# Attention with filler: the value products of two steps in one group, and the place of the maxima next to them

## The chip, the cores and the metric

The kernel runs on one core of a Trainium2 chip. The core has five engines with a queue each: TensorE (PE in the profile; its weight loads are shown as PEld), VectorE (DVE), ScalarE (ACT), GpSimd (POOL) and SyncE (SP, which here only issues DMAs). The metric is the device time of one execution in microseconds (us); less is better.

## The reference: what is computed

Four layers in turn on a sequence of 2048 rows of 448 numbers, each with a residual: attention, gated unit, attention, gated unit, with the same weights both times.

```python
x = x + A(layernorm(x)); x = x + B(layernorm(x)); x = x + A(layernorm(x)); x = x + B(layernorm(x))

def A(x):          # 16 query heads of 28, one key and value head for all
    q = (x @ wq) in 16 heads;  k = x @ wk;  v = x @ wv
    p = softmax(q k^T * 28 ** -0.5);  o = p v
    return o (heads side by side) @ wo
def B(x):          # F = 1792
    return (sigmoid(x @ w_gate) * (x @ w_up)) @ w_down
```

## The kernel before, in words

One attention and one gated unit make a *layer* of the kernel (`l` is 0 or 1). In a layer the queries are cut into 16 *units* of 128 rows (`u`), the keys into 16 blocks of 128 (`kt`). A **step** is one unit with one key block, so a layer has 256 steps, 16 to a unit. An order of letters, `ORDER` (line 901), says what a step issues, and in which order:

- `S`: `scores` (lines 506 to 514), four times a step, once for each group `g` of four heads. One matmul s of 96 rows into a bank of PSUM (L510), then ScalarE's exponential of it into an SBUF tile P of 128 x 512 in 32 bits (L513). Eight P tiles take turns.
- `P`: `pv` (lines 516 to 526): the products of the four P tiles of the *step before* with the values. Four matmuls stand side by side in four column strips of 32 (L521), all into one bank "pv" that sums over the 16 key blocks. Each of the four shows as two records in the profile, since the operands have 32 bits. After the last block of a unit ScalarE copies the bank out (L525).
- `M`: one step of `mx_gen` (lines 463 to 504), which works one unit ahead: four matmuls in four row strips of 32 (L480) and four reductions on VectorE (mp, L484), which give the maxima of the scores in advance. Once a unit, two small VectorE operations (L493, L494), a transpose on TensorE (mt, L499), a copy (L501) and a DMA on POOL's queue (L502) put the maxima into the query tile QS, from which the scores of the next unit are computed. It also issues the loads of QH and QS on SP.
- `X`: the side work of finished units (`tick`, stages f0 to ff of `Block.tile`, and db to df of `down`): the division by the sums with its DMAs, the product with wo (12 matmuls, L612), the layernorm, and in the first layer the keys and values of the next (kv). It also sets `rate`, the filler planned per step: what is left, over the steps until it must be done.
- `F`: `fill.slice(rate / number of F)`: filler from a generator, counted by a price per matmul (110 for the gated unit's gp and up, 190 for its down product dn, 216 for the query projection qp). The generator takes matmuls until the price is used up; side work (wo, kv) is charged to the same account, so after a wo some slices are empty. Each slice also issues deferred work (evictions on ScalarE and VectorE) that has become due.

The order of every engine's queue is the order of the program, so the letters set it. Between the layers, and after the last, a loop of filler slices with side work runs without scores. Scores, maxima, filler results and transposes share seven PSUM banks (tag "f", `fps`); a new tile takes the bank that was given back first. The eighth bank is pv's. A block of the gated unit is two units: it makes seven h tiles (`glu`, gp and up products, L345, tanh and products on ScalarE and VectorE), and then two down products read them. `HB` (ten) is the number of h tiles, and of the tiles with that tag that hold the first loads of x at the start (`load_x0`, line 794); `oT` (line 600) holds the divided output before wo, in two buffers.

Of the kernel before, what the change touches and what calls it, by code (L numbers as in the profile page):

```python
# [8 lines left out]
F32 = mybir.dt.float32  # L9
F16 = mybir.dt.float16  # L10
# [9 lines left out]
def interleaved_layers_kernel(ctx: ExitStack, tc: tile.TileContext, x, wq, wk, wv, wo, wg, wu, wd, out, layers=2):  # L20
# [7 lines left out]
    _, S, D = x.shape  # L28
    F = wg.shape[1]
    H, Dh = 16, 28  # L30
    NT, NB, G, KT, FC = S // 128, S // 512, H // 4, S // 128, F // 128
    U = NT
    TB, WB, HB = 2, 4, 10
    NBL = NT // TB
    EPS = 1e-5

# [5 lines left out]
    wk1 = ctx.enter_context(tc.tile_pool(name="wk1", bufs=2))  # L42
# [113 lines left out]
    def prep_q():  # L156
        parts = wk1.tile([128, 4], F32, name="parts", bufs=1)
        for c in range(4):
            junk = wk1.tile([128, D], F32, tag="P", name="junq", bufs=8)
            squares(parts[:, c:c + 1], rq[:, c], junk)  # L160
        nc.vector.tensor_reduce(mxa[:, 2:3], parts, axis=AX.X, op=OP.add)
        nc.vector.memset(WQ[:, :, :, :, Dh:32], 0.0)
        yield
        yield from scales(mxa[:, 2:3], 1, pwa[:, 2:3], swa[:, 2:3])
        for c in range(4):
            r = rq[:, c].rearrange("p (h d) -> p h d", d=Dh)
            split(WQ[:, 0, c, :, 0:Dh], WQ[:, 1, c, :, 0:Dh], r, swa[:, 2:3])
            yield
        nc.vector.tensor_scalar(esc, pwa[:, 2:3], pwa[:, 0:1], None, op0=OP.mult)
        nc.vector.tensor_scalar(esc, esc, Dh ** -0.5 * 2.0 ** -14, None, op0=OP.mult)  # L170
# [336 lines left out]
    def scores(l, u, kt, g, P):  # L507
        assert ("m", l, u) in stored, (l, u, kt)
        s = psf.tile([128, 512], F32, tag=BANKS["s"], name="s", bufs=NBK[BANKS["s"]])
        nc.tensor.matmul(s, KK[l][0:96, 0, kt * 128:(kt + 1) * 128], QS[l, u][:, g].rearrange("p h n -> p (h n)"),  # L510
                         start=True, stop=True)
        p = wk1.tile([128, 512], F32, tag="P", name="P", bufs=8)
        nc.scalar.activation(p, s, AF.Exp, scale=esc)  # L513
        P.append(p)

# [32 lines left out]
    class Block:  # L548
# [8 lines left out]
        def tile(self, u):  # L557

            l, b = self.l, self.b
            t = u % TB  # L560
            v = {}

            def f0():
                v["o"] = PVS.pop((l, u))
                nc.sync.dma_start(sums[u % 2], v["o"][28:128:32])
                v["xr"] = wk1.tile([128, D], F32, tag="xr", name="xr", bufs=4)
                nc.sync.dma_start(v["xr"], x[0, u * 128:(u + 1) * 128] if l == 0 else x2d[u])
                return
                yield

            def fx():
                v["rc"] = wk1.tile([128, 16], F32, name="rc")
                nc.sync.dma_start(v["rc"], sums[u % 2].rearrange("g (a b) -> (g a) b", b=16))
                return
                yield

            def fy():
                nc.vector.reciprocal(v["rc"], v["rc"])
                return
                yield  # L580

            def fz():
                nc.sync.dma_start(sums[u % 2].rearrange("g (a b) -> (g a) b", b=16), v["rc"])
                return
                yield

            def fw():
                lb = v["lb"] = wk1.tile([128, 512], F32, name="lb", bufs=1)
                for g in range(G):
                    nc.sync.dma_start(lb[32 * g:32 * g + 32], sums[u % 2][g:g + 1].to_broadcast([32, 512]))  # L590
                return
                yield

            def fa():
                nc.gpsimd.tensor_tensor(v["lb"], v["o"], v["lb"], op=OP.mult)  # L595
                return
                yield

            def fb():
                oT = v["oT"] = wk1.tile([128, 2, 512], F16, name="oT")  # L600
                nc.scalar.copy(oT[:, 0], v["lb"])
                defer(lambda: nc.vector.tensor_tensor(oT[:, 1], v["lb"], oT[:, 0], op=OP.subtract))  # L602
                return
                yield

            def fc():
                need(1)
                p = fps([128, D], F32, "wo")
                n = 0
                for h in range(4):  # L610
                    for a, c in ((0, 0), (0, 1), (1, 0)):
                        nc.tensor.matmul(p, v["oT"][:, a, h * 128:(h + 1) * 128], WO[:, c, h], start=n == 0, stop=n == 11)  # L612
                        n += 1
                        yield C448

                def f():
                    nc.vector.scalar_tensor_tensor(self.x1[:, t], p, osc, v["xr"], op0=OP.mult, op1=OP.add)
                    v["ls"] = ln_stats(self.x1[:, t])[0]
                defer(f)

            def fd():
                if t == TB - 1:
                    self.load_w(0)
                    self.load_w(1)
                v["hl"] = ln_split(self.x1[:, t], *v["ls"], eng=nc.gpsimd)
                return
                yield

            def fe():
                if t == 0:  # L630
                    self.XT2 = wk1.tile([128, 7, TB * 128], F16, name="XT2")
                t7_dma(v["hl"], self.XT2, t)
                return
                yield

            def ff():
                self.fed += 1
                if self.fed == TB:
                    fill.add(self.bulk(), BULK)
                    if b == NBL - 1 and not self.last:  # L640
                        fill.add(qgen(l + 1, 1), G * QCH)
                return
                yield
            return (1, f0), (1, fx), (1, fy), (1, fz), (1, fw), (1, fa), (1, fb), (2, fc), (2, fd), (3, fe), (2, ff)

        def load_w(self, f):
# [135 lines left out]
    fill = Filler()  # L782
# [115 lines left out]
        nmx += 1  # L898

    early[0] = False  # L900
    ORDER = "FSFSFSFSPXM"
    MORE = (5, 10)
    FIRST = KT * TB + 16
    KEEP = 28000
# [1 line left out]
    for l in range(layers):  # L906
        mx = mxs[l]
        final = l + 1 == layers
        if not final:
            layer_tiles(l + 1)  # L910
        if l:
            for b in range(2, NB):
                fill.add(qgen(l, b), G * QCH)
        fill.slice(QCH)
        flush(True)
        next(mx, None)
        while late:
            late.pop(0)[1]()
        fill.slice(QCH)
        prevP = None  # L920
        rate = 0.0
        for step in range(U * KT):
            u, kt = divmod(step, KT)
            P = []
            for o in ORDER:
                if o == "S":
                    scores(l, u, kt, len(P), P)
                elif o == "M":
                    for _ in range(1 + (u == 0 and kt in MORE)):
                        next(mx, None)  # L930
                elif o == "P":
                    if prevP is not None:
                        pv(*prevP)
                elif o == "X":
                    if u and kt == 1:
                        b = (u - 1) // TB
                        if (l, b) not in BLK:
                            BLK[l, b] = Block(l, b)
                        later(*BLK[l, b].tile(u - 1))
                    if l == 0:  # L940
                        paced(step)
                    tick()
                    fed = sum(BLK[l, b].fed == TB for b in range(NBL) if (l, b) in BLK)
                    if fed < NBL - 1:
                        rate = fill.left / max(FIRST + TB * KT * fed - step, 1)
                    else:
                        rate = max(fill.left - KEEP, 0) / (U * KT - step)
                else:
                    fill.slice(rate / ORDER.count("F"))
            prevP = (l, u, kt, P)  # L950
        pv(*prevP)
        flush(True)
        later(*BLK[l, NBL - 1].tile(U - 1))
        if not final:
            mxs[l + 1] = mx_gen(l + 1)
        n = done = 0
        while (side or pend or fill.gens) if final else (side or pend or done < 4 * NB):
            tick()
            for _ in range(4):
                fill.slice(VS / 4)  # L960
            n += 1
            if not final and done < 4 * NB and QDONE.get((l + 1, 0)) == G and mx_ready(l + 1, done):
                if n >= 5 or done >= 4 * (NB - 1):
                    next(mxs[l + 1])
                    done += 1
                    n = 0
# [21 lines left out]
```

## Time and profile before

| | before |
|---|---|
| median of 3 runs (lowest to highest) | 2358.69 us (2357.77 to 2359.82) |
| the profiled execution's own time | 2358.22 us |
| its span, first to last instruction | 2356.4 us |
| mean granted TensorE clock | 0.985 |
| filled steps, first layer | about 268 to 1144 us of the span |
| between the layers | about 1146 to 1275 us |
| filled steps, second layer | about 1425 to 2269 us |

Times in the profile count from the first instruction. A row of the timeline gives the start, the time from the first start to the last end, engine, line, operation, output and inputs, size and count; in brackets stands idle time before it and what ended it. A row of a window gives for each engine the busy time and, in brackets, the instructions, then the granted clock, the DMA engines' busy share and GB/s. Matmuls overlap in the array: one starts while the one before still drains, so the time that a matmul costs is read from start to start.

### The profile page before, as it was taken

What the parts mean: (1) busy time and instruction counts of PE and PEld (TensorE: products, weight loads), DVE (VectorE), ACT (ScalarE), POOL (GpSimd) and SP (SyncE); (2) the same over time, 40 slices, a digit from 0 to 9 for tenths busy, and PEclk for the clock granted to TensorE, in tenths of its full rate; (3) what the DMA queues carried; (4) which work ended last, traced back from release to release, by engine and by line L of the source; (5) the groups of instructions that cost most, each with busy time, mean ns of one, the idle gap of its engine ahead of it and who ended that gap; (6) DMA issues with size and microseconds to landing.
All of it is one profiled execution on the core that took longest, in us unless ns stands there. A gap on an engine that the chain in (4) does not pass through costs nothing.

```text
span 2356.4 us, 41206 instructions
## 1 busy us (share of the span) xinstructions
PE 2239.1 (95%) x15736; PEld 1003.2 (43%) x15736; DVE 1635.5 (69%) x2917; ACT 1559.2 (66%) x2598; POOL 336.8 (14%) x602
## 2 busy tenths in 40 slices
PE   5888899999999999999998989999999999999999
PEld 3322243444444444444572224444444444444456
DVE  6888787777777777773358877867676777777321
ACT  5588676776667677677413777767676776767751
POOL 5203763100110110001101011000000000000010
PEclk9799999999999999999998999999999999999999
DMA  3244652323313132333342112222231313223133
GB/s 114 65 126 124 201 190 81 90 73 98 96 58 109 58 93 70 94 92 78 96 139 53 27 49 92 87 78 83 62 103 58 98 55 101 76 82 94 57 111 119
DMA packets 208071, 213.88 MB, mean 91 GB/s; under 512 B 139952, under 2 KB 168304, under 8 KB 207872
## 3 DMA queue, kind: packets, MB, share of 16 engines
q1 hardware_dynamic: 202496, 196.36, 28.5%
q0 software_dynamic: 5376, 14.87, 1.8%
q8 instruction: 123, 2.02, 0.4%
q14 instruction: 76, 0.62, 0.1%
HBM read 175.37 MB, written 23.59 MB: 84 GB/s over the span
## 4 chain that ended last, share of the span: by engine, by line
PE 51%; DVE 5%; DMA 1%; ACT 1%; issue 0%; SPq 0%; POOL 0%; ACTq 0%; DVEq 0%; POOLq 0%
PE pv L521 12%; PE s L510 10%; PE dn L702 8%; PE gp L345 7%; PE up L345 7%; DVE mp L484 4%; PE mx L480 4%; PE wo L612 2%; PE qp L345 1%; ACT P L513 0%; DMA sums<-rc 0%; DMA KK<-ktl 0%; DMA rc<-sums 0%; DMA sums<-pvs 0%; DVE st L297 0%
## 5 line engine op out<-in xcount | busy, mean ns | idle before, releaser
L513 ACT ACTIVATE P<-s,esc 128x512 f32<-128x512 f32 x2048 | 1307.8, 690 | 509.2 <-PE s L510 492.1
L484 DVE TENSOR_REDUCE mp<-mx 128x1 f32<-128x512 f32 x2048 | 1267.2, 681 | 412.2 <-PE mx L480 408.1
L510 PE MATMUL s<-QS,KK 96*128 96x512 f16 x2048 | 761.1, 381 | 52.7 <-DVE mp L484 34.8
L345 PEld LDWEIGHTS <-wgu 128*128 128x128 f16 x4928 | 458.6, 98 | 241.3 <-issue 94.5
L521 PE MATMUL pv<-P,VV 128*32 128x512 f32 x4096 | 547.3, 607 | 0.0
L345 PE MATMUL up<-XT,wgu 128*128 128x256 f16 x2464 | 375.6, 272 | 0.8 <-DVE mp L484 0.8
L345 PE MATMUL gp<-XT,wgu 128*128 128x256 f16 x2464 | 375.2, 274 | 0.2
L702 PE MATMUL dn<-WD,h 128*128 128x448 f16 x1344 | 321.7, 352 | 0.0
L510 PEld LDWEIGHTS <-KK 96*128 96x128 f16 x2048 | 194.5, 97 | 172.1 <-issue 93.0
L480 PE MATMUL mx<-KK,QH 32*128 32x512 f16 x2048 | 223.2, 392 | 20.7 <-ACT QH L402 4.8
L480 PEld LDWEIGHTS <-QH 32*128 32x128 f16 x2048 | 53.5, 91 | 396.5 <-issue 378.1
L702 PEld LDWEIGHTS <-h 128*128 128x128 f16 x1344 | 124.1, 98 | 136.6 <-issue 22.6
L521 PEld LDWEIGHTS pv<-P,VV 128*32 128x32 f32 x4096 | 80.9, 108 | 204.4 <-issue 192.6
L595 POOL TENSOR_TENSOR lb<-pvs,lb 128x512 f32<-128x512 f32 x32 | 40.5, 1265 | 800.3 <-DMA lb<-sums 679.4
L676 ACT ACTIVATE h<-th 128x512 f16<-128x512 f32 x112 | 70.2, 627 | 86.4 <-DVE th L673 86.3
L345 PE MATMUL qp<-XT,WQ 128*128 128x512 f16 x352 | 114.5, 403 | 3.8 <-DVE mp L484 2.4
L673 DVE SCALAR_TENSOR_TENSOR th<-th,up 128x512 f32<-128x512 f32 x112 | 75.8, 677 | 59.0 <-PE up L345 46.5
L303 POOL TENSOR_SCALAR rs<-mv 128x1 f32<-128x1 f32 (+2 forms) x53 | 13.6, 256 | 686.4 <-DVE mv L298 682.9
L677 DVE SCALAR_TENSOR_TENSOR h<-th,h 128x512 f16<-128x512 f32 x112 | 77.7, 693 | 46.7 <-ACT h L676 46.7
L665 ACT ACTIVATE th<-gp,gsc 128x512 f32<-128x512 f32 x112 | 76.8, 685 | 47.7 <-PE gp L345 47.7
L612 PE MATMUL wo<-WO,oT 128*128 128x448 f16 x384 | 78.4, 353 | 0.3 <-DVE oT L602 0.2
L345 PEld LDWEIGHTS <-WQ 128*128 128x128 f16 x352 | 34.2, 101 | 64.2 <-issue 41.1
(126 smaller groups left out, 834.3 us busy)
## 6 DMA issues: line engine op xcount, KB each, us to landing
wgu<-wgu_d SPq DMA_DIRECT2D x224, 512.0 KB
QS<-qd SPq DMA_DIRECT2D x384, 32.0 KB
lb<-sums SPq DMA_DIRECT2D x128, 64.0 KB
xr<-in_A_x_dram SPq DMA_DIRECT2D x32, 224.0 KB
qd<-qst POOLq DMA_DIRECT2D x28, 256.0 KB, 2.7
wgu_d<-sgu POOLq DMA_DIRECT2D x14, 512.0 KB, 3.8
QH<-qd SPq DMA_DIRECT2D x28, 128.0 KB
x2d<-x SPq DMA_DIRECT2D x16, 224.0 KB
```

Source lines behind the costliest of these rows:

```text
L345: nc.tensor.matmul(ps, a, b, start=n == 0, stop=n == 10)
L480: nc.tensor.matmul(ps[h], qh[32 * h:32 * h + 32, g], KK[l][32 * h:32 * h + 32, 1, kb * 512:(kb + 1) * 512], start=True, stop=True, tile_po ...
L484: nc.vector.tensor_reduce(mp[:, g, h, kb:kb + 1], ps[h], axis=AX.X, op=OP.max)
L510: nc.tensor.matmul(s, KK[l][0:96, 0, kt * 128:(kt + 1) * 128], QS[l, u][:, g].rearrange("p h n -> p (h n)"), start=True, stop=True)
L513: nc.scalar.activation(p, s, AF.Exp, scale=esc)
L521: nc.tensor.matmul(v[32 * g:32 * g + 32], VV[l][:, kt], P[g], start=kt == 0, stop=kt == KT - 1, tile_position=(0, 32 * g))
L612: nc.tensor.matmul(p, v["oT"][:, a, h * 128:(h + 1) * 128], WO[:, c, h], start=n == 0, stop=n == 11)
L665: defer(lambda: nc.scalar.activation(th, gp.rearrange("p j n -> p (j n)"), AF.Tanh, scale=gsc))
L673: nc.vector.scalar_tensor_tensor(t, th, 1.0, up.rearrange("p j n -> p (j n)"), op0=OP.add, op1=OP.mult)
L676: nc.scalar.activation(h[:, 0], t, AF.Copy, scale=2.0 ** -17)
L677: defer(lambda: nc.vector.scalar_tensor_tensor(h[:, 1], t, 2.0 ** -17, h[:, 0], op0=OP.mult, op1=OP.subtract), 1)
L702: nc.tensor.matmul(p, hs[f // 2][:, a, o:o + 128], WD[:, f, c], start=n == 0, stop=n == 3 * FC - 1)
```

## The change

Two orders, taken by turns, replace `ORDER` where the planned filler is over 800 a step; the old order stays for the other steps. In the even step of a pair all pending value products (those of two steps) stand behind the second score, and the maxima right behind them; in the odd step there are no value products, and the maxima stand behind the third score. The side work moves to the end of the step. Twelve P tiles instead of eight hold what is pending; for that room two of ten h tiles and one of two oT tiles are given up.

```diff
-    TB, WB, HB = 2, 4, 10
+    TB, WB, HB = 2, 4, 8
...
-            junk = wk1.tile([128, D], F32, tag="P", name="junq", bufs=8)
+            junk = wk1.tile([128, D], F32, tag="P", name="junq", bufs=12)
...
-        p = wk1.tile([128, 512], F32, tag="P", name="P", bufs=8)
+        p = wk1.tile([128, 512], F32, tag="P", name="P", bufs=12)
...
-                oT = v["oT"] = wk1.tile([128, 2, 512], F16, name="oT")
+                oT = v["oT"] = wk1.tile([128, 2, 512], F16, name="oT", bufs=1)
...
-    ORDER = "FSFSFSFSPXM"
+    FULL = ("FSFSPMFSFSX", "FSFSFSMFSX")
+    POOR = "FSFSFSFSPXM"
+    ENOUGH = 800
...
-        prevP = None
+        pend_p = []
...
-            for o in ORDER:
+            order = FULL[kt % 2] if rate > ENOUGH else POOR
+            for o in order:
...
-                    if prevP is not None:
-                        pv(*prevP)
+                    while pend_p:
+                        pv(*pend_p.pop(0))
...
-                    fill.slice(rate / ORDER.count("F"))
-            prevP = (l, u, kt, P)
-        pv(*prevP)
+                    fill.slice(rate / order.count("F"))
+            pend_p.append((l, u, kt, P))
+        while pend_p:
+            pv(*pend_p.pop(0))
```

## The prediction

> **What bounds the kernel now.** I read the page first, for the engines and the chain.
>
> ```profile
> span 2356.4 us, 41206 instructions
> PE 2239.1 (95%) x15736; PEld 1003.2 (43%) x15736; DVE 1635.5 (69%) x2917; ACT 1559.2 (66%) x2598; POOL 336.8 (14%) x602
> ...
> PE 51%; DVE 5%; DMA 1%; ACT 1%; issue 0%; SPq 0%; POOL 0%; ACTq 0%; DVEq 0%; POOLq 0%
> ```
>
> TensorE (PE) is busy 95% of the span, and no other engine has more than 5% of the chain that ended last. The change touches only steps in which filler runs beside the attention, so the next view is the sums over the two filled stretches (one a layer), then the same windows for the instructions of pv and of mx alone, then what TensorE waited for in the second stretch.
>
> ```profile
> 268.00:1144.20 876.20, 855.90 (x6163) 387.57 (x6160) 620.32 (x1101) 617.58 (x1012) 148.48 (x259) 1.00 0.33 96
> 1425.00:2268.60 843.60, 834.57 (x5990) 379.02 (x5993) 581.53 (x998) 598.85 (x957) 60.83 (x131) 1.00 0.27 81
> ```
>
> ```profile
> 268.00:1144.20 876.20, 223.55 (x1672) 32.92 (x1672) 7.63 (x13) 1.00 0.33 96
> 1425.00:2268.60 843.60, 222.78 (x1676) 32.96 (x1680) 7.61 (x13) 1.00 0.27 81
> ```
>
> ```profile
> 268.00:1144.20 876.20, 76.23 (x764) 474.13 (x767) 1.00 0.33 96
> 1425.00:2268.60 843.60, 75.32 (x764) 474.74 (x766) 1.00 0.27 81
> ```
>
> ```profile
> PE s L510 <- DVE mp L484: 8.2, 25, 0.5
> ```
>
> The first pair of rows has busy time of PE, weight loads, DVE, ACT, POOL: PE 98 to 99%, DVE 69 to 71%, ACT 70 to 71%; the granted clock is 1.00. In the second stretch all that TensorE visibly waits for is 8.2 us. So here TensorE's own sequence sets the time, and what shortens it counts one for one until another engine falls behind. A step issues 8 pv records (4 products in 2 passes): 1672 + 1676 make 418.5 filled steps. mx has 4 a step: 1528 make 382, so some 36 filled steps, the last ones of each layer, have no mx.
>
> **The change, part by part.** Its core is read from the order on TensorE in one plain filled step (start, us).
>
> ```profile
> 1570.71 0.38 PE L510 MATMUL s<-QS,KK 96*128 96x512 f16 x1
> 1571.02 1.06 PE L521 MATMUL pv<-P,VV 128*32 128x512 f32 x8
> 1572.02 0.39 PE L480 MATMUL mx<-KK,QH 32*128 32x512 f16 x4
> 1572.35 0.50 PE L345 MATMUL up<-XT,wgu 128*128 128x256 f16 x3
> 1572.68 0.38 PE L510 MATMUL s<-QS,KK 96*128 96x512 f16 x1
> 1572.90 0.60 PE L345 MATMUL up<-XT,wgu 128*128 128x256 f16 x4
> 1573.34 0.38 PE L510 MATMUL s<-QS,KK 96*128 96x512 f16 x1
> ...
> 1574.86 1.06 PE L521 MATMUL pv<-P,VV 128*32 128x512 f32 x8
> ```
>
> Starts tell more than durations, since matmuls are pipelined. A score before filler holds TensorE 0.22 us (1572.68 to 1572.90), a score before pv 0.31 (1570.71 to 1571.02): entering the column-tiled pv costs 0.09. The pv group takes 1.00 until mx starts, mx 0.33 until the filler starts, a step 3.84 (1571.02 to 1574.86). The seven filler matmuls between 1572.35 and 1573.34, less one score, are 0.11 each.
>
> *Two groups together.* The trace has this operation already: after the last step of a layer two pv groups stand side by side.
>
> ```profile
> 1143.91 0.38 PE L510 MATMUL s<-QS,KK 96*128 96x512 f16 x1
> 1144.22 1.92 PE L521 MATMUL pv<-P,VV 128*32 128x512 f32 x16
> 1146.08 0.39 PE L345 MATMUL gp<-XT,wgu 128*128 128x256 f16 x2
> ```
>
> Sixteen records take 1.86 us to the next start, two single groups 2 x 1.00 = 2.00: 0.14 less. The other step of the pair now goes from a score straight to mx. The trace does not show that in a filled step; from below it costs the plain 0.22, from above (a score before the other tiled form) 0.31, and since both are changes of tiling I take 0.31, the cost of the score-to-pv change that it replaces. So a pair saves 0.14 us. 3348 pv records / 16 are 209 pairs, less one at the start of the filled part of a layer: 208 x 0.14 = **29.1 us**. The code chooses the new order where the planned filler is over 800 a step: the step above has 14 matmuls of 110, 1540. The poor steps have one or two of 216 (below), so they keep the old order.
>
> ```profile
> 139.25 0.38 PE L345 MATMUL qp<-XT,WQ 128*128 128x512 f16 x1
> ```
>
> The Trainium skill, "TensorEngine Tiling", section Key Properties, says that changing the tiling mode, unlike changing the tile, drains TensorE. The rows agree: 0.09 us at each change. By that rule alone a pair goes from six changes to five and saves 0.09, which would make 18.7 us in place of 29.1; the row of sixteen decides here, because it measures the whole operation.
>
> *Steps without mx.* With no mx, the odd step has no change of tiling at all: a pair saves 0.09 more (score before filler 0.22 for 0.31). 36 steps are 18 pairs: **1.6 us**.
>
> *Side work.* The old order has it between pv and mx, the new one at the end of the step, between fillers.
>
> ```profile
> 1468.59 2.44 PE L612 MATMUL wo<-WO,oT 128*128 128x448 f16 x12
> 1470.96 0.39 PE L480 MATMUL mx<-KK,QH 32*128 32x512 f16 x4
> 1471.29 0.39 PE L510 MATMUL s<-QS,KK 96*128 96x512 f16 x1
> 1472.13 0.38 PE L510 MATMUL s<-QS,KK 96*128 96x512 f16 x1 [0.45 <-DVE mp L484]
> 1472.72 0.59 PE L510 MATMUL s<-QS,KK 96*128 96x512 f16 x2 [0.22 <-DVE mp L484]
> ```
>
> ```profile
> 1551.41 0.74 PE L702 MATMUL dn<-WD,h 128*128 128x448 f16 x3
> 1551.98 0.38 PE L510 MATMUL s<-QS,KK 96*128 96x512 f16 x1
> ```
>
> The 12 wo matmuls hold TensorE 2.37 us; three of the same size among fillers take 0.57, so twelve would take 2.28. One change of tiling, 0.09, goes. There is one wo a unit of 16 steps, 26 in 418 steps, and in the first layer one kv a unit, 13: 39 x 0.09 = **3.5 us**.
>
> *The step after wo.* Its fillers are used up, four scores come in a row and wait for maxima (1471.29 to 1472.72: 1.43 for two, 1.0 us over 0.44). It is an even step. In the new order its first two scores and a double pv follow wo, then mx; but two scores, hardly a filler and the next step's scores stand before the next mx, so VectorE has about as little time as now. I cost it at nothing; it could give back all 1.0 in 26 units, or take 0.2 more: -26 to +5.
>
> *The maxima.* VectorE's cover gets thinner: mx came every 3.84 us; now the distance alternates. From an even step's mx to an odd one's there are five fillers, four scores at 0.22 and one before mx at 0.31. With 14 fillers of 0.11 a step, 0.33 + 17.5 x 0.11 + 0.88 + 0.31 = 3.44 us; the other way the rest of the pair, 2 x 3.84 - 0.14 - 3.44 = 4.10.
>
> ```profile
> 1572.44 2.48 DVE L484 TENSOR_REDUCE mp<-mx 128x1 f32<-128x512 f32 x4 [1.35 <-PE mx L480]
> ...
> 1608.51 0.67 DVE L673 SCALAR_TENSOR_TENSOR th<-th,up 128x512 f32<-128x512 f32 x1
> ...
> 1609.95 2.48 DVE L484 TENSOR_REDUCE mp<-mx 128x1 f32<-128x512 f32 x4
> ```
>
> ```profile
> 1608.59 0.40 PE L480 MATMUL mx<-KK,QH 32*128 32x512 f16 x4
> ```
>
> The four reductions end 2.90 us after the mx of 1572.02: 0.54 before 3.44. All scores, mx and fillers draw on seven banks; with one held by a filler the reuse is six tiles back, so the odd mx waits for the even one's fourth reduction, with 0.54 to spare. Other VectorE work queued ahead can make reductions later (1609.95 + 2.48 is 3.84 after an mx at 1608.59), but what is issued after an mx stands behind its reductions, so it delays only the next mx's, and before an even mx there are now 4.10 us, not 3.84. I add 3 us, from 0 to 20 (0.1 a pair).
>
> *The transpose of the maxima (mt)* falls in the 14th step of a unit (kt 13, by counting four scores to a step), an odd one, and needs two small VectorE operations behind the previous mx's reductions.
>
> ```profile
> 1550.05 1.06 PE L521 MATMUL pv<-P,VV 128*32 128x512 f32 x8
> 1550.93 0.22 PE L499 MATMUL mt<-id,m 128*16 128x128 f16 x1
> 1551.08 0.39 PE L480 MATMUL mx<-KK,QH 32*128 32x512 f16 x4
> ```
>
> ```profile
> L493 DVE TENSOR_REDUCE m<-mp 128x16 f32<-128x64 f32 x32 | 6.7, 210 | 0.5
> L494 DVE TENSOR_SCALAR m<-m 128x16 f16<-128x16 f32 x32 | 6.6, 205 | 1.1
> ```
>
> It stood 0.88 after pv's start, it now stands directly behind a score, about 3.3 us after the previous mx, where reductions end at 2.90 and the two operations (0.21 each) at 3.3 plus handover. I add 0.15 a unit, 26 x 0.15 = 4 us (0 to 10). Who waits behind it is TensorE itself.
>
> *Moved DMAs.* Of mx move the loads of QH and QS (SP) and the store of the maxima's row into QS (POOL's queue), of the side work its loads and stores (SP), each within one step of 3.84 us and past the other in SP's queue. The QH and QS loads are for the next unit; the row is stored at kt 13 and read by the first score three steps, some 11 us, later; the stages of the side work stand a step or more apart. Nothing; if a store came late, the first score of a unit would wait.
>
> *Buffers.* Twelve P tiles cover the most that are held, ten (eight of two steps and two scores); the exponentials are released as before. oT with one buffer is written once a unit, some 60 us apart: nothing. Seven of the eight h tiles are one block's; the next block's second one is written 88 matmuls of 0.11 after the last down product: nothing. At the start only eight tiles of x, not ten, are fetched ahead. The ninth load now waits, on SP's queue, for POOL to finish tile 0; its statistics run at 17.12.
>
> ```profile
> 11.66 0.90 POOL L316 TENSOR_TENSOR hl<-xr,hl 128x384 f16<-128x384 f32 x1
> ```
>
> ```profile
> 17.12 0.61 DVE L816 BATCH_NORM_STATS2 st<-xr 128x6 f32<-128x448 f32 x1
> ```
>
> That leaves 4.5 us (12.56 to 17.12) for the transfer: nothing, at most about 1.5.
>
> **The sum** is made against the profiled execution's own 2358.2 (span 2356.4 and 1.8 around it; the median of the runs is 2358.7, 0.5 above). -29.1 - 1.6 - 3.5 = -34.2, +3 + 4 = -27.2: forecast **2331**.
>
> **The rivals.** *VectorE becomes the bound (slower).* Between even and odd mx VectorE needs 2.90 of 3.44 us; one operation of 0.67 ahead of the even reductions, with two fillers holding banks (reuse five back, spare 0.2), stalls the odd step 0.47. For it speaks 1609.95; against it DVE at 69% in that stretch and only 8.2 us of waits. In half the pairs, 104 x 0.47 = 49 us, it gives 2358 - 34 + 49 = 2373; it turns the sign from 73 pairs up (34.2 / 0.47). The Trainium skill, "TensorEngine Tiling", section PSUM Bottleneck, warns of the same: tiling speeds up TensorE but not the emptying of PSUM, which may become the limit. Here no filled stretch shows it yet.
> *Stalls eat about half:* 0.08 a pair, 17 us: 2341 to 2350. *The sequence gains more:* the step after wo loses its stall, -26 with no new waits: 2298 to 2310. *It does not do what it says:* if the planned filler were over 800 only in half the steps, 17 us: 2341; the counted 1540 speaks against it.
>
> **How the numbers follow.** Forecast's case (2318 to 2341) 0.62; half eaten or half applied 0.16; more gained 0.10; no change 0.05; VectorE the bound 0.07. 2310 to 2352 leaves out most of the third and the last case, and some of the first's luck. A measurement here tells 0.2% (4.7 us) from no change: faster 0.87, same 0.05, slower 0.08.
>
> **What would show it.** pv in runs of sixteen, 1.86 to the next start, every second filled step, and scores 0.31 before mx in the others; pv's busy time down from 547 by about 208 x 0.2; the filled stretches shorter by some 14 us each, the poor ones and the layer change as before. Wrong would be: waits of scores or mx for mp several times 8.2 us in the second stretch, a score before mx far over 0.31, or a late first layer.

## The result, and the profile after

| | before | after |
|---|---|---|
| median of 10 runs each (lowest to highest), us | 2359.26 (2356.70 to 2363.36) | 2365.01 (2358.74 to 2366.93) |
| ratio to before, 95% interval | 1 | 1.0018 (1.0009 to 1.0026) |
| profiled execution's own time, us | 2358.22 | 2363.80 |

The changed kernel is 0.18% slower. The forecast of 2331, its range and its sign were wrong: 34 us were forecast to go, and nothing of them is seen in the total.

The page of after begins so; the second fence, from the page's groups, has the two kinds of instructions that were moved (busy, mean ns, then idle time ahead of them).

```profile
span 2362.0 us, 41187 instructions
PE 2237.8 (95%) x15736; PEld 1029.5 (44%) x15736; DVE 1647.9 (70%) x2917; ACT 1553.4 (66%) x2598; POOL 337.9 (14%) x602
...
PE 78%; DVE 12%; ACT 3%; issue 1%; DMA 1%; SPq 1%; POOL 0%; DVEq 0%; ACTq 0%; POOLq 0%
```

```profile
L521 PE MATMUL pv<-P,VV 128*32 128x512 f32 x4096 | 506.9, 604 | 0.0
...
L480 PE MATMUL mx<-KK,QH 32*128 32x512 f16 x2048 | 253.7, 391 | 36.3 <-ACT P L513 16.5
```

The same groups of before:

```profile
L521 PE MATMUL pv<-P,VV 128*32 128x512 f32 x4096 | 547.3, 607 | 0.0
...
L480 PE MATMUL mx<-KK,QH 32*128 32x512 f16 x2048 | 223.2, 392 | 20.7 <-ACT QH L402 4.8
```

pv lost 40.4 us of busy time, where the prediction named 208 x 0.2 = 41.6: the pairs are there. But mx gained 30.5 busy and 15.6 idle, 46.1 in all, for the same 2048 matmuls of the same 0.39. A group of four whose last one waits shows partly as a longer busy stretch (0.54 instead of 0.40), partly as idle time; only the sum of both tells. The releaser is new too: ScalarE's exponential (P, L513).

A plain pair on TensorE in after (timeline):

```profile
1568.37 0.38 PE L510 MATMUL s<-QS,KK 96*128 96x512 f16 x1
1568.68 1.92 PE L521 MATMUL pv<-P,VV 128*32 128x512 f32 x16
1570.54 0.40 PE L480 MATMUL mx<-KK,QH 32*128 32x512 f16 x4
1570.86 0.50 PE L345 MATMUL up<-XT,wgu 128*128 128x256 f16 x3
...
1573.61 0.38 PE L510 MATMUL s<-QS,KK 96*128 96x512 f16 x1
1573.92 0.40 PE L480 MATMUL mx<-KK,QH 32*128 32x512 f16 x4
```

This is the pair that was forecast: sixteen records in 1.86, 0.31 from the score to mx, 3.38 from one mx to the next. In some 80 of the 207 pairs mx runs without a wait, as here. The loss lies in the others. For all runs I add up, from the starts in the trace, by how much each matmul of an mx group starts later than 3 ns behind the one before it, where that is over 25 ns, over the steps 47 to 253 of each layer (a step begins with its first score). Call these the **waits inside mx**. A short one is up to 0.5 us, a long one over that. Beside them stand the two filled stretches, from step 47 to step 254.

| | waits inside mx, us: short (count) | long (count) | sum | filled, layers 1 and 2, us |
|---|---|---|---|---|
| before | 0.3 (2) | 0.7 (1) | 1.0 | 867.6, 835.2 |
| after | 22.5 (107) | 26.4 (26) | 48.9 | 858.4, 841.6 |

All of after's are in odd steps, and 46.9 of the 48.9 us are at the group's *fourth* matmul. A long one in after, from the timeline of all engines:

```profile
1487.11 0.40 PE L480 MATMUL mx<-KK,QH 32*128 32x512 f16 x4
...
1487.53 2.48 DVE L484 TENSOR_REDUCE mp<-mx 128x1 f32<-128x512 f32 x4 [2.12 <-PE mx L480]
...
1489.09 0.38 PE L510 MATMUL s<-QS,KK 96*128 96x512 f16 x1
...
1489.93 0.68 DVE L673 SCALAR_TENSOR_TENSOR th<-th,up 128x512 f32<-128x512 f32 x1
...
1490.64 0.63 ACT L676 ACTIVATE h<-th 128x512 f16<-128x512 f32 x1 [1.05 <-DVE th L673]
...
1490.71 0.39 PE L480 MATMUL mx<-KK,QH 32*128 32x512 f16 x3
1491.18 2.47 ACT L513 ACTIVATE P<-s,esc 128x512 f32<-128x512 f32 x4
...
1491.90 0.37 PE L480 MATMUL mx<-KK,QH 32*128 32x512 f16 x1 [0.79 <-ACT P L513]
```

Read it from below. The fourth mx matmul starts 1.19 after the group, 1.17 late (0.79 of it shows as idle time), when the first of four exponentials in a row is done. That exponential, of the score of 1489.09, could not start before 1491.18, because ScalarE's queue stood at the rounding of h (L676, the 16-bit part of a finished filler result) and that waited 1.05 us for VectorE's product th (L673). th in turn stood in VectorE's queue behind the four reductions of the even mx. Fifteen of the 26 long waits (17.1 us) are of this kind. Five more (5.6 us, first layer) stand behind another rounding at the head of ScalarE's queue, hl (L314) of the layernorm, which waits for VectorE's xn (L322). A short one has no such chain:

```profile
1463.49 0.68 ACT L665 ACTIVATE th<-gp,gsc 128x512 f32<-128x512 f32 x1
...
1463.70 0.38 PE L510 MATMUL s<-QS,KK 96*128 96x512 f16 x1
...
1464.06 2.42 ACT L513 ACTIVATE P<-s,esc 128x512 f32<-128x512 f32 x4
...
1465.21 0.54 PE L480 MATMUL mx<-KK,QH 32*128 32x512 f16 x4
```

The odd step's first score is at 1463.70, its mx 1.51 later. A tanh of 0.68 had held ScalarE up, and the exponential of the score before came first, so this score's is the second of the four in a row and ends at about 1465.33. The fourth mx matmul starts at 1465.38, 0.16 late; the mean short wait is 0.21.

Not all short waits are for ScalarE. After a wo there are few fillers, and the odd mx stands only 2.62 behind the even one:

```profile
1471.19 0.40 PE L480 MATMUL mx<-KK,QH 32*128 32x512 f16 x4
...
1471.61 3.31 DVE L484 TENSOR_REDUCE mp<-mx 128x1 f32<-128x512 f32 x5 [1.04 <-PE mx L480]
...
1473.81 0.71 PE L480 MATMUL mx<-KK,QH 32*128 32x512 f16 x4
```

Here the fourth matmul waits 0.31 for the fourth reduction of the even mx, which ends at about 1474.09. Each waiting matmul names in the trace the semaphore (a counter that another engine raises) that it waits for, and each of them starts 50 to 55 ns after an instruction that raises it has ended. Sorted by that instruction, the waits of after are:

| waited for | short, us (count) | long, us (count) |
|---|---|---|
| ScalarE, exponential of a score (P, L513) | 8.9 (45) | 25.3 (24) |
| ScalarE, tanh of a filler result (th, L665) | 1.9 (9) | none |
| VectorE, reduction of the even mx (mp, L484) | 6.1 (22) | none |
| VectorE, copy of the transposed maxima (mr, L501) | 4.3 (12) | none |
| VectorE, other evictions (th L673, qst L412) | 1.3 (19) | 1.1 (2) |

So ScalarE accounts for 36.1 us, VectorE for 12.8, and VectorE for half of the short ones. The 22 for a reduction are all at kt 11, the step after the one that follows wo, the 12 for the copy all at kt 13, where mt stands directly ahead of mx.

Why the fourth: in the program's own order of the seven banks (odd steps 48 to 235 of both layers, 188 of them) the fourth mx matmul takes the bank of the *same* step's first score 92 times, of its second 31 times; the third takes one of these two 94 times, the second 8 times, the first never. The bank alone does not decide, since the third matmul waits for only about 2 us in all: the exponential must be late as well. In the order of before a pv group of 1.00 us stands between the last score and mx.

### The profile page after: what moved, and what is told of

Read it like the earlier page. It is cut to its first block, busy times and chain, and to the rows that moved or that the text cites. A ratio compares the mean times of both kernels' runs of the same rounds, so it can differ in the third digit from the quotient of the medians.

```text
span 2362.0 us, 41187 instructions
## 1 busy us (share of the span) xinstructions
PE 2237.8 (95%) x15736; PEld 1029.5 (44%) x15736; DVE 1647.9 (70%) x2917; ACT 1553.4 (66%) x2598; POOL 337.9 (14%) x602
## 3 DMA queue, kind: packets, MB, share of 16 engines
q1 hardware_dynamic: 202496, 196.36, 28.7%
## 4 chain that ended last, share of the span: by engine, by line
PE 78%; DVE 12%; ACT 3%; issue 1%; DMA 1%; SPq 1%; POOL 0%; DVEq 0%; ACTq 0%; POOLq 0%
PE pv L521 19%; PE s L510 16%; PE dn L702 11%; PE up L345 11%; DVE mp L484 9%; PE gp L345 9%; PE mx L480 7%; PE wo L612 3%; ACT P L513 2%; PE qp L345 2%; DVE h L677 1%; DMA sums<-rc 0%; ACT h L676 0%; PE mt L499 0%; DVE st L297 0%
## 5 line engine op out<-in xcount | busy, mean ns | idle before, releaser
L513 ACT ACTIVATE P<-s,esc 128x512 f32<-128x512 f32 x2048 | 1305.9, 691 | 506.9 <-PE s L510 491.4
L484 DVE TENSOR_REDUCE mp<-mx 128x1 f32<-128x512 f32 x2048 | 1269.8, 683 | 418.0 <-PE mx L480 413.3
L510 PE MATMUL s<-QS,KK 96*128 96x512 f16 x2048 | 761.0, 383 | 40.4 <-DVE mp L484 23.4
L521 PE MATMUL pv<-P,VV 128*32 128x512 f32 x4096 | 506.9, 604 | 0.0
L480 PE MATMUL mx<-KK,QH 32*128 32x512 f16 x2048 | 253.7, 391 | 36.3 <-ACT P L513 16.5
L521 PEld LDWEIGHTS pv<-P,VV 128*32 128x32 f32 x4096 | 103.2, 109 | 258.9 <-issue 247.5
L676 ACT ACTIVATE h<-th 128x512 f16<-128x512 f32 x112 | 70.2, 627 | 85.5 <-DVE th L673 85.5
L673 DVE SCALAR_TENSOR_TENSOR th<-th,up 128x512 f32<-128x512 f32 x112 | 75.6, 675 | 63.9 <-PE up L345 48.1
L677 DVE SCALAR_TENSOR_TENSOR h<-th,h 128x512 f16<-128x512 f32 x112 | 81.5, 728 | 42.0 <-ACT h L676 42.0
L665 ACT ACTIVATE th<-gp,gsc 128x512 f32<-128x512 f32 x112 | 76.8, 686 | 41.7 <-PE gp L345 41.6
```

Of the source, the lines that this page charges most:

```text
L480: nc.tensor.matmul(ps[h], qh[32 * h:32 * h + 32, g], KK[l][32 * h:32 * h + 32, 1, kb * 512:(kb + 1) * 512], start=True, stop=True, tile_po ...
L484: nc.vector.tensor_reduce(mp[:, g, h, kb:kb + 1], ps[h], axis=AX.X, op=OP.max)
L521: nc.tensor.matmul(v[32 * g:32 * g + 32], VV[l][:, kt], P[g], start=kt == 0, stop=kt == KT - 1, tile_position=(0, 32 * g))
L665: defer(lambda: nc.scalar.activation(th, gp.rearrange("p j n -> p (j n)"), AF.Tanh, scale=gsc))
L673: nc.vector.scalar_tensor_tensor(t, th, 1.0, up.rearrange("p j n -> p (j n)"), op0=OP.add, op1=OP.mult)
L676: nc.scalar.activation(h[:, 0], t, AF.Copy, scale=2.0 ** -17)
```

## The experiments

**The theory:** the waits inside mx eat the pairs' gain, and they are waits for ScalarE to empty the banks of scores of the same step. **Rivals:** VectorE's reductions are too slow for the shorter distance (the prediction's own rival), the smaller buffers cost the time, or the moved side work does. After the first eight runs the theory took a second form: short waits because the exponential is simply too recent, long ones because ScalarE's queue is held by the rounding of h.

### The buffers alone

```diff
# to before: HB 10 -> 8, P and junq bufs 8 -> 12, oT bufs 1; the order unchanged
```


> The kernel before with the buffers of the change alone: 12 P tiles, 8 h tiles, one oT tile, order unchanged. Theory: no effect, 2356 to 2362, ratio to before within 0.2%. Rival (the smaller buffers cost the gain): 2385 or more, since the sequence alone was worth 34 us.

2359.84 (10 runs), 0.9998 (0.9986 to 1.0011): the buffers cost nothing. That rival is gone.

### Shorter reductions

```diff
-  nc.vector.tensor_reduce(mp[:, g, h, kb:kb + 1], ps[h], axis=AX.X, op=OP.max)
+  nc.vector.tensor_reduce(mp[:, g, h, kb:kb + 1], ps[h][:, 0:256], axis=AX.X, op=OP.max)
```


> The changed kernel with reductions over 256 of 512 columns, so half of the keys are left out of the maxima and VectorE has about 1.1 us less per step. Theory (ScalarE empties score banks late): waits inside the odd maxima group stay, above 35 of 49 us; what goes are only the waits of scores for reductions (some 10 to 20 us, poor steps more), so 2330 to 2350. Rival (VectorE): the waits inside the maxima group go almost wholly, under 10 us, and the time falls to 2310 or less.

2272.95 (one run). The groups of this kernel for VectorE and TensorE:

```profile
L484 DVE TENSOR_REDUCE mp<-mx 128x1 f32<-128x256 f32 x2048 | 723.8, 416 | 715.0 <-PE mx L480 710.2
```

```profile
L480 PE MATMUL mx<-KK,QH 32*128 32x512 f16 x2048 | 244.8, 389 | 23.3 <-ACT P L513 7.4 <-DMA KK<-ktl 4.4 <-ACT QH L402 4.2
```

A reduction takes 416 ns in the mean where after's page has 683. The total fell by 91 us, about half of it in the poor steps and at the start (44 us); the expectation of the total had left that out. Up to 14 of the 44 us come from less time at half clock there (31 us in this execution, 58 in that of after). The waits inside mx are 29.4 us: short ones 21.1 (107 of them, as in after), long ones 8.3 (13) instead of 26.4. The long ones fall, as th comes out of VectorE's queue earlier. The equal number of short ones hides an exchange: those for a reduction went from 6.1 us to none, those for an exponential rose from 8.9 to 14.8. Part of that is not the reductions' doing, since this program deals out the banks differently (the fourth mx matmul takes the bank of the same step's first score 122 times, not 92). With 24.7 of the 29.4 us left for ScalarE when no reduction is waited for any more, VectorE's reductions fall as the main cause; they were the cause of about 6 us, and for the long ones VectorE is one link.

### Shorter exponentials

```diff
-        p = wk1.tile([128, 512], F32, tag="P", name="P", bufs=12)
-        nc.scalar.activation(p, s, AF.Exp, scale=esc)
+        p = PT[npt[0] % 12]          # 12 tiles set to 1.0 once
+        npt[0] += 1
+        nc.scalar.activation(p[:, 0:256], s[:, 0:256], AF.Exp, scale=esc)
```


> The changed kernel, but each exponential covers 256 of 512 columns; the P tiles are twelve standing tiles, filled with ones once, whose other half is never written, so half of the queries get no attention. ScalarE has some 0.27 us less per score, VectorE the same. Theory (ScalarE empties the score bank too late for the fourth maxima matmul): the waits inside the odd maxima group fall from 49 us to under 12 and the filled stretches lose 35 us or more against the changed kernel (858 and 842): 2325 to 2335 in all. Rival (VectorE late): they stay above 35 us.

2314.18 (one run), waits inside mx 24.7: short 6.7 (50), long 18.0 (19). Now the short waits go and the long ones mostly stay: those short ones that are for an exponential fall from 8.9 us to 3.5. It is no clean cut, though: the banks are dealt out differently here too, and the short waits for VectorE fall as well, from 11.7 us to 2.6. The expected "under 12" was a miss, since the first form of the theory had no long kind. The filled stretches are 33.5 us shorter than in after, more than the 24.2 of mx, so ScalarE is short of time elsewhere too.

### The rounding of h on GpSimd

```diff
-  nc.scalar.activation(h[:, 0], t, AF.Copy, scale=2.0 ** -17)
+  nc.gpsimd.tensor_scalar(h[:, 0], t, 2.0 ** -17, None, op0=OP.mult)
```


> The changed kernel with the high half of h rounded on GpSimd instead of ScalarE: 112 operations of 0.63 us leave ScalarE's queue. Theory (ScalarE late): those of the waits inside the odd maxima group that stand behind such an operation go, 49 us to 25 to 38; time about 2345 to 2358. Rival (VectorE): the waits stay at 45 or more; time 2360 to 2368.

2379.91 (one run). Long waits 8.0 (9) instead of 26.4, short ones 22.4 as in after: with the rounding of h out of ScalarE's queue, its long blocks go. Of the 8.0 left, 5.6 (5) stand behind the other rounding, hl. The total got worse, because GpSimd takes 1.49 us for what ScalarE does in 0.63, and VectorE, which then needs h (L677), is held up with its reductions behind:

```profile
L676 POOL TENSOR_SCALAR h<-th 128x512 f16<-128x512 f32 x112 | 167.2, 1493 | 750.5 <-DVE th L673 749.5
```

```profile
L510 PE MATMUL s<-QS,KK 96*128 96x512 f16 x2048 | 758.8, 381 | 69.2 <-DVE mp L484 52.9 <-ACT P L513 12.6 <-DMA QS<-mr 0.7
```

Scores waited 23.4 us for mp in after, 52.9 here. For the total this run settles nothing; the split of the waits is what it shows.

### The rounding of h two slices later

```diff
-                    defer(parts, 2)
+                    defer(parts, 4)
```


> The changed kernel with ScalarE's rounding of h issued four filler slices after its product instead of two, so that VectorE has done that product, behind its four reductions, before ScalarE comes to it. Theory in its second form (two kinds of wait at the odd step's fourth maxima matmul: about 95 short ones of 0.2 us, where the bank's score is simply recent, and about 24 long ones of 1.0 us, where the exponential stands in ScalarE's queue behind a rounding of h that waits for VectorE): the long ones go, 49 us to 20 to 30, total 2336 to 2346. Rival (the long waits come from ScalarE's load, not from the blocked head of its queue): no change, 49 us, 2362 to 2367.

2347.95 (4 runs), 0.9954 (0.9939 to 0.9969): a gain of some 15 us on after by the two ratios. The waits fell to 37.1: short 21.1 (108), as in after, long 16.0 (23) instead of 26.4. The long ones were expected to go, so the total missed too. The trace shows what happened: the 15 waits behind a rounding of h that itself waits (17.1 us) are gone, and in the second filled stretch ScalarE no longer waits for th at all (24 times in after). In place of them there are eleven, 6.2 us together, where the rounding, now ready, stands in the row ahead of the exponential and is simply work; at 0.5 to 0.6 us each they count as long. The five behind hl stay (5.6 us). So the second form had this mechanism right, and the sum wrong: it took all long waits for one kind.

### Place alone

```diff
-    FULL = ("FSFSPMFSFSX", "FSFSFSMFSX")
+    FULL = ("FSFSPMFSFSX", "FSFSPMFSFSX")
```


> The new place alone: products every step (one group, as before), the maxima right behind them after the second score, side work at the end of the step (F S F S P M F S F S X in every filled step). Theory: nothing of the pair's 29 us, but no waits inside the maxima group either (under 5 us), since the products stand ahead of them; the side work saves 3.5 us: 2350 to 2360. Rival (VectorE): 2352 to 2362 too, so this run tells only whether the place by itself costs.

No pairs: each step has its products and maxima behind the second score and the side work at its end. 2339.29 (4 runs), 0.9920 (0.9906 to 0.9935), better than either theory had it. The waits inside mx are 0.8 us, and the TensorE waits of the second filled stretch (1435 to 2230 us) are one line:

```profile
PE s L510 <- DVE mp L484: 4.8, 14, 1.0
```

In after the same view has three:

```profile
PE mx L480 <- ACT P L513: 9.5, 12, 0.8
PE s L510 <- DVE mp L484: 5.5, 16, 0.9
PE mt L499 <- DVE m L494: 2.0, 6, 0.3
```

So the change holds two things of opposite worth. The new place, side work included, gives -0.80%, and with that the moved side work is no cause of the loss; the pairs on top of it cost 0.98%, some 23 us (1.0018 against 0.9920, each a ratio to before in its own series). ScalarE's blocks are in this kernel too (it waits 25 times in this stretch for th, in after 24 times), but with a pv group ahead of mx they hurt nobody.

### Pairs at the old place

```diff
+    FULL = ("FSFSFSFSPXM", "FSFSFSFSXM")
```


> Pairing alone: value products of two steps in every second filled step, everything else at its old place (F S F S F S F S P X M, and F S F S F S F S X M without products). The pair still saves 0.14 us on TensorE (29 us). Theory: in the odd step the maxima stand directly behind the fourth score and have no products ahead of them, so their last matmul waits for ScalarE as in the changed kernel: waits inside the odd maxima group 40 us or more, total 2355 to 2370. Rival (VectorE's uneven distance is what costs): here the distance from the even to the odd maxima is about 3.1, shorter than in the changed kernel, and the waits are those of scores and maxima for reductions, over 60 us, total 2380 or more.

2390.32 (4 runs), 1.0138 (1.0123 to 1.0153): the pairs alone cost 33 us. Waits inside mx 37.5, of which 28.7 short; 20.6 of the 37.5 are for VectorE, 15.6 for ScalarE. The distance from an even to an odd mx is now shorter still, and here VectorE is late as well: the transpose of the maxima waits for it in the first filled stretch (273 to 1150 us) as follows, and by 6.6 us in the second.

```profile
PE mt L499 <- DVE m L494: 11.3, 12, 2.1
```

The total lies in the rival's range, the waits inside mx in neither's (40 or more, over 60). Both mechanisms are real; in after ScalarE's is the larger, with 36.1 of 48.9 us.

### Where the odd step's maxima stand

Three places in the odd step, the even one unchanged:

```diff
+    FULL = ("FSFSPMFSFSX", "FSFSFSFMSX")     # one slice after the third score
+    FULL = ("FSFSPMFSFSX", "FSFSFFMSFSX")    # two slices after the second score
+    FULL = ("FSFSPMFSFSX", "FSFSFSFFMSX")    # two slices after the third; defer(parts, 4)
```


> The odd step's maxima stand one filler slice later, behind score, filler instead of directly behind the third score (order F S F S F S F M S X). Theory (the fourth maxima matmul waits until ScalarE has emptied the bank of a score issued about 1.5 us before): a slice more, some 0.4 us, lets most of these waits go; the waits inside the maxima group in the filled stretches fall from 49 us to under 20, and the time to about 2335 (2325 to 2345). First rival (VectorE's reductions of the even step are the late ones): the distance even to odd grows too, so it gives about the same here; it is told apart by the run with short reductions. Second rival (fewer buffers): 2365, no change.

> The odd step's maxima behind the second score and two filler slices (F S F S F F M S F S X). The bank of the fourth matmul was last used by a score some 0.3 us longer ago than when they stand directly behind the third score; VectorE gets about 3.3 us from the even maxima, 0.1 less. Theory: waits inside the maxima group 15 to 30 us, total 2338 to 2350, like the run with one slice before. Rival (VectorE): less distance, so as slow as the changed kernel or slower, 2362 to 2375.

> As the run before, with two slices between the third score and the odd step's maxima (F S F S F S F F M S X). Theory: waits inside the maxima group under 6 us; the fourth score directly behind may wait instead: 2318 to 2334. Rival: no better than one slice, 2330 to 2346.

The first: 2345.48 (4 runs), 0.9944 (0.9928 to 0.9961), waits 26.5 (short 6.6, long 19.9), the right direction, but short of what was expected (under 20): one slice of filler between score and mx takes most of the short waits away, those for VectorE too (1.2 us of 12.8 left), and leaves most of the long ones. The second: 2356.63 (10 runs), 0.9991 (0.9981 to 1.0001), waits only 5.6, and yet hardly a gain, so that both expectations were missed: what no longer waits in mx waits in the score behind it, for the same ScalarE (its waits in the second filled stretch, and the score's group over the whole run, where after has 14.1 us for ScalarE and 23.4 for VectorE):

```profile
PE s L510 <- ACT P L513: 10.3, 12, 0.9
PE s L510 <- DVE mp L484: 6.6, 22, 0.7
```

```profile
L510 PE MATMUL s<-QS,KK 96*128 96x512 f16 x2048 | 760.1, 382 | 62.7 <-ACT P L513 31.0 <-DVE mp L484 26.9 <-DVE qst L412 1.0
```

The third (its "run before" is the one with both cures, below): 2346.00 (4 runs), 0.9947 (0.9932 to 0.9962), at the end of the rival's range; waits 14.3 instead of the few expected, and the scores behind mx start late by 12.7 us in the filled stretches (1.8 in before). A wait that was moved off mx came back, in part, at the next matmul that needed a bank.

### Both cures, and the best version

```diff
+    FULL = ("FSFSPMFSFSX", "FSFSFSFMSX")     # pairs, one slice later;  defer(parts, 4)
+    FULL = ("FSFSPMFSFSX", "FSFSPMFSFSX")    # no pairs, place alone;   defer(parts, 4)
```


> The same rounding of h four slices later, and the odd step's maxima one slice later (F S F S F S F M S X). Theory: the first removes the long waits, the second most of the short ones: under 12 us inside the maxima group, total 2322 to 2334, below the place alone (2339). Rival (the two remedies remove the same waits): 2338 to 2346.

> The new place alone (single product groups every step, maxima behind them) with the rounding of h four slices later. Theory: there were no waits inside the maxima group, so only a few us of waits of scores for reductions can go: 2332 to 2342. Rival (the later rounding is worth 20 us by itself, whatever the order): 2315 to 2325.

Pairs with both cures: 2343.19 (4 runs), 0.9937 (0.9922 to 0.9952), waits 17.8; that is the rival's range, not the theory's. Place alone with the later rounding: **2333.99** (4 runs), 0.9892 (0.9873 to 0.9910), waits 0.7, as expected and the fastest of all.

### Six banks instead of seven

```diff
-    NBK = {"f": 7, "s": 2, "m": 3}
+    NBK = {"f": 6, "s": 2, "m": 3}
```


> The changed kernel with six PSUM banks in turn instead of seven. Theory (the odd maxima's matmuls need banks that scores of the same step have just used, about 0.2 us too early in half the pairs): with one bank fewer the third and fourth matmul get the banks of scores one place later in the step, some 0.6 us more recent, so the waits inside the maxima group grow from 49 us to 130 or more, the total to 2430 or more. Rival (banks are not what these waits are for; ScalarE's or VectorE's queues alone set them): 45 to 70 us, total 2362 to 2390.

> The new place alone with six banks in turn. Theory: where the product group stands ahead of the maxima, 1.0 us lies between the last score and the maxima, so inside the maxima group little is waited for (under 15 us) and the loss is that of scores waiting for reductions: 2345 to 2385, far less lost than by the paired order. Rival: the loss of a bank costs both orders the same.

After with six: 2470.37 (one run); place alone with six: 2435.58 (one run). Their mx groups:

```profile
L480 PE MATMUL mx<-KK,QH 32*128 32x512 f16 x2048 | 304.0, 390 | 43.5 <-ACT P L513 22.9 <-DVE mp L484 6.4 <-DMA QH<-qd 3.9
```

```profile
L480 PE MATMUL mx<-KK,QH 32*128 32x512 f16 x2048 | 246.1, 393 | 22.1 <-DVE mp L484 6.8 <-DMA QH<-qd 4.1 <-ACT QH L402 3.6
```

The waits inside mx go from 48.9 to 103.3 with the pairs, and from 0.8 to 20.3 without. So banks are what mx waits for, and it needs them more with the pairs (+54 us against +20). The expected 130 was not reached, though, and the second total is far over what was expected: the totals rise by 105 and 96 us, so most of a lost bank's price is paid elsewhere, by the scores and the poor steps, in either order. In the totals the second run's rival, the same price for both orders, is nearly right.

## Why the prediction was wrong, point by point

Over the filled stretches I also add up every start of a matmul of mx, s, filler or side work, and of a pv group, that comes over 25 ns later than the plain distance for its kind and its neighbour's (0.22 from a score on, 0.11 from gp or up on, and so on). Before has 48.1 us of such **late starts**, after 75.5, place alone 25.9. Those of mt, counted apart, are 4.1 us in before and 7.5 in after. The stretches measure 858.4 + 841.6 - 867.6 - 835.2 = -2.8 where -27.2 was forecast. Late starts account for +27.4 and mt for +3.4, which leaves -33.6 for the sequence itself (34.2 forecast). So TensorE's own sequence came out as forecast, and the waits ate it: mx gained 47.9 us of them, and all others together lost 20.5.

- *Two groups together, 29.1:* right. A pair without late starts in the second layer (kt 14 and 15 of every second unit) takes 5.25 + 3.39 where before had 4.39 + 4.39: 0.14 less, as forecast, and a score before mx takes the 0.31 that was assumed.
- *Steps without mx, 1.6, and side work, 3.5:* as forecast where seen. A pair without mx went from 6.69 to 6.45 us in layer 2, 0.24 less (0.14 + 0.09 forecast). After's wo holds TensorE 2.27 to the next start, 0.10 less than 2.37.
- *The step after wo, costed at nothing:* mis-sized. The step with wo and the one behind it took, in the mean of ten units of layer 2 (the fifth to the fourteenth), 5.94 + 3.29 us before, 5.00 + 3.55 after, 5.90 + 2.69 with the place alone. Less 0.13 for the pair and 0.09 for the side work, after gains 0.46 a unit, the place alone 0.55 (less 0.09): 12 to 14 us in 26 units. Late starts of a score behind a score fell from 23.9 to 9.7. It lay inside the bounds (-26 to +5), nearer to the end that I did not take: the products now stand behind two of the scores that waited in a row, and the others wait less. Without this gain, which the sum did not count on, the change would have lost more.

```profile
1598.24 2.43 PE L612 MATMUL wo<-WO,oT 128*128 128x448 f16 x12
1600.51 0.60 PE L510 MATMUL s<-QS,KK 96*128 96x512 f16 x2
1601.04 1.92 PE L521 MATMUL pv<-P,VV 128*32 128x512 f32 x16
1602.89 0.40 PE L480 MATMUL mx<-KK,QH 32*128 32x512 f16 x4
```

- *The maxima, "3 us, from 0 to 20":* **the step that failed.** It asked what the odd mx waits for, answered "the even one's fourth reduction", and found 0.54 us to spare. That was one bank of four. A group of four needs four banks at once, and in 123 of 188 odd steps the fourth was last held by a score of the same step, which ScalarE has to empty. With the pv group ahead of mx the banks had 1 us more; without it one of them came late, by 0.2 us in the mean of 107 short waits and by 1.0 in that of 26 long ones. The price was 48, not 3 and not 20: 36 for ScalarE, which this step of the prediction did not ask about, and 13 for VectorE, 6.1 of it for the very reduction that was named, at kt 11, where the distance is 2.62 and not 3.44.
- *The rival "VectorE becomes the bound":* its place (the odd mx) fits, and its size (49 us) by luck, since its mechanism carries a small part. 12.8 of the 48.9 us are for VectorE, and only 6.1 for the reductions that the rival is about; the larger part is for ScalarE, with VectorE also as the link ahead of the two roundings. The warning of the Trainium skill, "TensorEngine Tiling (Array Packing)", section PSUM Bottleneck, came true in its general form: TensorE ends up waiting for PSUM to be emptied, with 48.9 us in this trace. It is the order that does it here, since the place alone has the same tiling and 0.8 us. Which engine empties too late is something only the trace tells.
- *mt, 4:* mis-sized, though inside its range (0 to 10). The two steps around mt (kt 12 and 13) took, in the mean of the same ten units, 8.28 before and 8.63 after in layer 2, 8.99 and 9.07 in layer 1, where a clean pair saves 0.13: 0.35 a unit in the mean of both layers, 9 us in 26 units. 3.4 us of it are mt's own later start; 4.3 are the waits of the fourth mx matmul for the copy of mt's result, which nobody had asked about, and they are part of the 48.9 above.
- *Moved DMAs, buffers:* right, nothing: no wait of TensorE for a load or store of QS shows in after, and the buffers have their own run.
- *Poor steps:* "as before" was not quite what the two profiles show. Steps 0 to 47 and the first 48 of layer 2 take 176.2 and 158.8 us, where before had 170.5 and 156.0, 8.5 more with the order unchanged. The profiled execution with the buffers alone, whose median is that of before, has 174.7 and 158.7, so the change doesn't explain it; more stretches at a lower clock fell into them. The granted clock was 0.5 for 6.8 us of these steps in before, for 23.9 in after and also with the buffers alone; half of the difference between before and after is 8.5. The windows before the first and before the second filled stretch, of before and of after (the third column from the right is the granted clock):

```profile
100.00:268.00 168.00, 146.80 (x850) 38.38 (x849) 135.36 (x236) 139.93 (x251) 47.76 (x55) 0.98 0.46 134
...
1275.00:1425.00 150.00, 134.82 (x808) 33.94 (x808) 125.77 (x216) 113.45 (x190) 13.49 (x26) 1.00 0.14 41
```

```profile
100.00:268.00 168.00, 146.35 (x828) 37.45 (x826) 133.46 (x231) 139.21 (x249) 44.54 (x52) 0.96 0.45 131
...
1275.00:1425.00 150.00, 135.33 (x793) 33.57 (x792) 124.45 (x213) 110.56 (x184) 12.74 (x25) 0.98 0.14 39
```

What stays open: the medians of after and before differ by 5.8 us, the filled stretches by -2.8. The rest lies in the poor steps of the two profiled executions, where the half clock accounts for it. Whether a median execution of after has as much of it is not shown: the profiled one with the buffers alone lies 7.4 us above its own median, after's 1.2 below. So why after is slower than before, and not about the same, stays open in part; where the pairs' gain went does not.

## What to carry to other kernels

When a group of work moves, list for *each* buffer that it needs who held it last, which engine empties it and when, not only for the one that came to mind: a group that takes four buffers at once waits for the worst of four. Work that stands between a producer and the next user of the buffers is also time for another engine; before taking it away, ask who used that time. A split of waits by whom they wait for says more than their sum: in one run here the short waits kept their number while their cause changed. And take a change with two parts apart: here the place was worth 0.8%, the pairs cost more than that, and the sum looked like nothing.

## What the runs showed of the hardware that was not expected

- Queues in the order of the program link work that shares no data: the fourth matmul of TensorE's maxima started 1.17 us late for a filler product of VectorE that it doesn't need, by way of a rounding that stood at the head of ScalarE's queue for 1.05 us and of a bank.
- In the poor steps the granted clock drops to 0.5 for stretches of 3.4 or 6.8 us at a time, although it is at 1.00 through the filled ones (but for one such stretch at 591 us in before). A pv group in one of them in after takes 1.74 instead of 1.06:

```profile
1288.69 1.74 PE L521 MATMUL pv<-P,VV 128*32 128x512 f32 x8
```

- The same rounding of 128 x 512 numbers from 32 to 16 bits takes 1.49 us on GpSimd and 0.63 on ScalarE.
